# Moving the conversions of a weight matrix between steps of a one-core attention and soft-MoE kernel

## The chip, the cores and the metric

The program runs on one core of a Trainium2 chip. The metric is the device time of one execution in microseconds (us). The kernel before was run three times; its median is 592.17 us (591.44 to 594.74).

## The reference, cut to what matters

```python
# attention: batch 4, heads 12, sequence 448, head dimension 64
scores = cap * np.tanh(scale * np.matmul(q, k.transpose(0, 1, 3, 2)) / cap)
scores = scores - np.max(scores, axis=-1, keepdims=True)
attn = np.exp(scores)
attn = attn / (np.sum(attn, axis=-1, keepdims=True) + 1e-09)
x = (attn @ v) as 1792 tokens x 768
# soft mixture of experts: 8 experts, 4 slots each, 768 -> 1024 -> 768
logits = x @ phi                                  # 1792 x 32
d = softmax of logits over the tokens
slot_input = d.T @ x
slot_out = per expert: np.maximum(slot_input[e] @ w1[e], 0.0) @ w2[e]
x = (softmax of logits over the slots) @ slot_out # 1792 x 768
# MLP: 768 -> 2048 -> 768
h = x @ w_in
g = np.maximum(h, 0.0) + alpha * np.minimum(h, 0.0)
out = g @ w_out
```

The matrices w_in and w_out are stored with 64 bits per number, so the kernel reads each number as two 32-bit words, `lo` and `hi`, and rebuilds a float32 from them.

## The kernel before, in words

**Attention in steps.** Two heads make a pair, so there are 24 pairs. Each pair has four steps, one per block of keys, so the loop runs over steps `g` = 0 to 95 (and two more to drain); `c = g % 4` is the step within the pair. A step issues on TensorE (PE) the score products `s` of one block (six matmuls from the split operands `qh`, `ql`, `kh`, `kl`), then on ScalarE (ACT) a tanh (line 388) and an exp (line 389), and two steps later the product with v (tile `o`). GpSimd (POOL) adds up the exponentials into `acc` (lines 405, 408, 412), six instructions per pair.

**What is prepared ahead.** In the second step of a pair (`c == 1`) the next pair's k and q are transposed on PE (tile `tr`). From the result in PSUM, ACT writes `kh` (line 353), and VectorE (DVE) writes `qh`, `kl` and `ql` (lines 367, 354, 368). Besides that come, as background work due some steps later, the row sums (`rs` on PE, lines 439 and 443 on DVE), every third pair a reciprocal (lines 469 to 471: RECIPROCAL, a cast, and `rh`), the normalisation (`rb` on PE, `xn` on DVE, line 495), the logits (`lg`), the two softmaxes, transposes of x (`nx` on PE, `xnat` on DVE or ACT) and the slot sums (`ss`). The tiles `tr`, `rs`, `rb`, `lg`, `lr`, `nx`, `nd` and `ss` all come out of one PSUM pool of three buffers that are used in rotation: the next one on PE waits until the reader of the third last has done.

**w_in's conversion.** w_in is cut into 24 pieces of 128 by 512 numbers. A piece is loaded by DMA as 64-bit words (512 KB) into one of two buffers of the tile `cvbuf`, rebuilt there by one instruction on ACT (line 185) and four on DVE, and stored to a scratch array (256 KB, line 688) two steps after its conversion; after the store the load of the piece after next is issued (line 668). At which step `g` a piece is converted stands in the list `cv_steps`. The four instructions on DVE are

```python
nc.vector.tensor_scalar(out=t, in0=t, scalar1=H_MIN, scalar2=H_MAX, op0=ALU.max, op1=ALU.min)       # L186
nc.vector.tensor_scalar(out=tu, in0=tu, scalar1=4, scalar2=1, op0=..., op1=...)                      # L190
nc.vector.scalar_tensor_tensor(out=tu, in0=lo, scalar=29, in1=tu, op0=..., op1=...)                  # L193
nc.vector.scalar_tensor_tensor(out=tu, in0=hi, scalar=0x80000000, in1=tu, op0=..., op1=...)          # L196
```

so L186 and L190 read one array, L193 and L196 read two. `order` fixes the order on PE; L185 and L186 are held back until their step. A scheduler arranges the rest of each engine's instructions.

**Expert weights.** While attention runs, `load_next` fetches the first expert weights into slots of a shared area, at the pairs listed in `LOADS`. The eleventh load goes into the slot that `cvbuf` occupies, and so waits for the last store of w_in.

**After attention** come the eight experts, and the MLP with w_in and w_out, both bound to PE.

Of the kernel before, what the change touches and what calls it, by code (L numbers as in the profile page):

```python
# [24 lines left out]
def tile_attention_soft_moe_mlp(ctx, tc, q, k, v, cap, phi, w1, w2, w_in, w_out, alpha, out):  # L25
    nc = tc.nc
    B, H, S, D = q.shape
    J = 4
    P = S // J
    NP = H // 2  # L30
    NPAIR = B * NP
# [8 lines left out]
    HS = S // 2  # L40
# [13 lines left out]
    LOADS = (4, 6, 8, 10, 12, 14, 16, 18, 19, 20, 21, 22)  # L54
# [22 lines left out]
    def slot(i, shape, dtype=F32, name="w"):  # L77
        return arena.tile(shape, dtype, tag=f"slot{i}", name=name)
# [18 lines left out]
    def may_load():  # L97
        if nload[0] == len(loads):
            return None
        late = loads[nload[0]][0] in ("wi", "wo")  # L100
        fit = [n for n in free if not late or n < NA]
        return fit[0] if len(fit) > (late and not kept[0]) else None

    def w1_rows(e, i):

        return w1[e, 384 * i:384 * i + 384, :].rearrange("(p k) f -> p k f", k=3)

    def w2_rows(e, i):

        return w2[e, 512 * i:512 * i + 512, :].rearrange("(j p u) f -> p j u f", p=128, u=2)  # L110

    def load_part(kind, e, i, c, t, after=None):
        if kind == "w2":
            src = w2_rows(e, i)[:, c // 2, c % 2]
        else:
            src = w1_rows(e, i)[:, c]
        ins = nc.sync.dma_start(out=t, in_=src)
        if after is not None:
            tc.add_manual_dep(ins.ins, after.ins.name, NOSYNC, reason="prefetch pace")
        return t  # L120

    def load_next(after=None):
        slot_no = may_load()
        free.remove(slot_no)
        kind, e, i = loads[nload[0]]
        nload[0] += 1
        if slot_no >= NA:

            ts = where.setdefault((kind, e, i), [])
            n = 3 if kind == "w1" else 4  # L130
            for c in range(len(ts), n):
                t = xslots[0].tile([128, SLOT // n], F32, tag=f"slot{slot_no}_{c}", name="w")
                ts.append(load_part(kind, e, i, c, t))
            return
        if kind == "w1":
            t = slot(slot_no, [128, 3, FE])
            src = w1_rows(e, i)
        elif kind == "w2":
            t = slot(slot_no, [128, 4, DM])
            src = w2_rows(e, i)  # L140
        elif kind == "wi":
            t = slot(slot_no, [128, KD, 512])
            src = w_in32[i].rearrange("(k p) f -> p k f", p=128)
        else:
            t = slot(slot_no, [128, 2, DM, 2], U32)
            src = w_out[256 * i:256 * i + 256].rearrange("(k p) f t -> p k f t", p=128)
        if kind == "w1":
            parts = [(t, src)]
        elif kind == "w2":
            parts = [(t[:, 2 * j:2 * j + 2], src[:, j]) for j in range(2)]  # L150
        else:
            parts = [(t[:, c], src[:, c]) for c in range(t.shape[1])]
        if kind == "wo" and i == 0:

            half.append(parts.pop())
        elif kind == "wi" and i == 0:
            parts = [
                (t[:, ks, fs], src[:, ks, fs])
                for fs in (slice(0, 256), slice(256, 512))
                for ks in (slice(0, 3), slice(3, 6))  # L160
            ]
            parts[2:2] = half
        for dst, part in parts:
            ins = nc.sync.dma_start(out=dst, in_=part)
            if after is not None:
                tc.add_manual_dep(ins.ins, after.ins.name, NOSYNC, reason="prefetch pace")
        if kind == "w1":
            t = [t[:, c] for c in range(3)]
        elif kind == "w2":
            t = [t[:, c] for c in range(4)]  # L170
        where[kind, e, i] = t
        held[kind, e, i] = slot_no
# [61 lines left out]
    def attention():  # L234
        with ExitStack() as pools:
# [27 lines left out]
            phi_sb = ac0_p.tile([128, KD, NSLOT], F32, name="phi")  # L263
# [13 lines left out]
            nat, stk, sc_t, pt, acc, ov, xu, xn = {}, {}, {}, {}, {}, {}, {}, {}  # L277
# [7 lines left out]
            def matmul(*a, **kw):  # L285
                ins = nc.tensor.matmul(*a, **kw)  # L286
                if order:
                    if order[0] is not None:
                        tc.add_manual_dep(ins.ins, order[0].ins.name, NOSYNC, reason="tilings together")
                    order[0] = ins  # L290
                return ins
# [8 lines left out]
            def aux(shape, name):  # L300
                if now[0] > NPAIR * J and name in ("nx", "ss"):
                    return ps_s.tile([128, 2, 512], F32, tag="s", name=name)[:, 0, :][:shape[0], :shape[1]]
                return ps_a.tile([128, 512], F32, tag="a", name=name)[:shape[0], :shape[1]]
# [212 lines left out]
            def logits(b, part):  # L516

                if part != 1:
                    lps[b] = aux([128, S], "lg")
                ps = lps[b]  # L520
                pairs = range(NP) if part is None else range(GP) if part == 0 else range(GP, NP - 1)
                end = pairs.stop if part != 0 else NP - 1
                for m in pairs:
                    r = 32 * (m % 4)
                    matmul(
                        ps[r:r + 32, :],
                        phi_sb[:, m, :],
                        xn[b * NP + m],
                        start=(m < 4),
                        stop=(m + 4 >= end),  # L530
                        tile_position=(0, r),
                    )
                if part == 0:
                    return
                ls = sm_p.tile([128, S], F32, tag="ls", name="ls")
                if part is None:
                    nc.vector.tensor_copy(out=ls, in_=ps)
                else:
                    nc.scalar.activation(out=ls, in_=ps, func=AF.Copy)
                if part is None:  # L540
                    later(2, softmax_d, b, ls)
                    for m in range(2):
                        later((2 if b < B - 2 else 4) + m, nat_x, b * NP + m)
                    return
                norm(NPAIR - 1, sums[NPAIR // GP - 1], True)
                for m in range(5):
                    nat_x(b * NP + m)
                lps[b] = aux([128, S], "lr"), ls
                matmul(lps[b][0], stackI, ls, start=True, stop=False)
                for m in range(3):  # L550
                    nat_x(b * NP + m)
                last_logits()
# [117 lines left out]
            ncv = KD * (DFF // 512)  # L670


            cv_steps = [4, 7, 10, 13, 16, 19, 22, 25, 29]
            while len(cv_steps) < ncv:
                cv_steps.append(cv_steps[-1] + J)

            def cv_at(n):
                return cv_steps[n]
# [39 lines left out]
            last = None  # L718
            for g in range(NPAIR * J + LAG):
                now[0] = g  # L720
                i, c = divmod(g, J)
                if g == 14:
                    nc.sync.dma_start(out=alpha_sb, in_=alpha.rearrange("(k p) -> p k", p=128))
                if g == 17:
                    nc.vector.tensor_scalar(out=nalpha_sb, in0=alpha_sb, scalar1=-1.0, scalar2=None, op0=ALU.mult)
                if i < NPAIR:
                    qk(i, CHUNKS[c])
                    if c == 1 and i + 1 < NPAIR:
                        trans_k(i + 1)
                        trans_q(i + 1)  # L730
                run_bg()
                if i < NPAIR:
                    if c == 0:
                        last = load(i + 2, "kq") or last
                    for n in range(ncv):
                        if cv_at(n) == g - 2:
                            store_w_in(n)
                        if cv_at(n) == g:
                            conv_w_in(n)
                    if c == 3 and i in LOADS and may_load() is not None:  # L740
                        load_next(last)
                if g >= LAG:
                    n, e = divmod(g - LAG, J)
                    pv(n, CHUNKS[e])
                    if e == J - 1:
                        load(n + 2, "v")
            order.clear()
            while bg:
                now[0] += 1
# [8 lines left out]
            ps = aux([128, KD * NSLOT], "si").rearrange("p (k s) -> p k s", k=KD)  # L758
# [611 lines left out]
```

## Time and profile before

| | before |
|---|---|
| median of three runs | 592.17 us (591.44 to 594.74) |
| the profiled execution | 591.62 us |
| its span | 589.7 us |
| mean granted clock of TensorE | 0.991 |
| PE busy | 94% of the span |
| DVE, ACT, POOL busy | 74%, 64%, 29% |

The span is what the profiler recorded of the program; the execution's own time is 1.9 us longer. Busy shares are averages over three stages of different kind: attention (to about 255 us), experts, MLP. POOL works in attention alone. The pairs are counted from 0. Pair p's stretch is taken from the start of its first tanh to that of the next pair, and the windows below have these borders: pair 2 begins at 28.27 us, pairs 3, 4 and 5 at 36.44, 46.32 and 56.52, pair 6 at 66.63, pair 13 at 133.16, pair 21 at 217.24 and pair 23 at 238.65.

### The profile page before, as it was taken

The page shows a single profiled execution, that of the slowest core. Times are in us where ns is not written, and L with a number is a line of the kernel's source. Part 1 is how long each engine was busy: PE and PEld are TensorE (multiplying, and loading weights), DVE is VectorE, ACT ScalarE, POOL GpSimd, SP SyncE. Part 2 cuts the span into 40 slices and gives each one's busy share as a digit, 9 for nine tenths or more (in the row PEclk, how much of TensorE's full clock was granted, in tenths as well). Part 3 has the DMA queues.
Part 4 walks back from the last instruction along what each step waited for, and adds up shares of the span by engine and source line. Part 5 has one row for each costly group of instructions (what it writes and reads, how often), then busy time and mean ns, then how long its engine had stood idle before and what let it go on. Part 6 is the DMA issues. An engine that isn't in the chain of part 4 may idle for free.

```text
span 589.7 us, 10780 instructions
## 1 busy us (share of the span) xinstructions
PE 557.1 (94%) x4008; PEld 385.1 (65%) x4008; DVE 437.7 (74%) x834; ACT 377.0 (64%) x617; POOL 173.1 (29%) x158
## 2 busy tenths in 40 slices
PE   5998999999999999989888899999999999999996
PEld 4443444445444545454445568878888999999996
DVE  3699798896769768451012399999999979797974
ACT  3997999798988878620011167764787855555651
POOL 0799588767585755500000000000000000000000
PEclk9999999999999999997999999999999999999999
DMA  7668788798887971899999999300120101010101
GB/s 177 128 183 285 197 241 260 211 241 260 245 246 197 323 233 51 306 360 412 419 421 418 391 400 416 116 0 1 42 67 1 55 0 54 2 53 1 54 1 54
DMA packets 83460, 110.92 MB, mean 188 GB/s; under 512 B 55376, under 2 KB 63312, under 8 KB 81872
## 3 DMA queue, kind: packets, MB, share of 16 engines
q1 hardware_dynamic: 81168, 109.28, 55.9%
q10 hardware_dynamic: 2240, 0.95, 0.6%
q8 instruction: 32, 0.52, 0.4%
q14 instruction: 20, 0.16, 0.1%
HBM read 98.41 MB, written 11.80 MB: 187 GB/s over the span
## 4 chain that ended last, share of the span: by engine, by line
PE 78%; DVE 9%; ACT 6%; DMA 3%; issue 2%; SPq 1%; ACTq 0%; DVEq 0%
PE o L286 9%; PE s L286 8%; PE P L1196 7%; PE P L1194 6%; PE P L1195 6%; PE oc L969 6%; PE oc L975 6%; PE oc L976 6%; PE y L860 5%; PE h L836 4%; PE aps L897 2%; PE nx L286 2%; ACT p L389 2%; PE rs L286 2%; ACT p L388 2%
## 5 line engine op out<-in xcount | busy, mean ns | idle before, releaser
L286 PE MATMUL o<-p,v 128*64 128x448 f32 (+1 forms) x384 | 94.0, 568 | 3.2 <-ACT xu L414 2.6
L388 ACT ACTIVATE p<-s 128x896 f32<-128x896 f32 x96 | 78.6, 819 | 23.7 <-PE s L286 20.7
L389 ACT ACTIVATE p<-p,cap 128x896 f32<-128x896 f32 x96 | 91.0, 948 | 2.2
L405 POOL TENSOR_TENSOR acc<-p 128x448 f32<-128x448 f32 x48 | 60.1, 1273 | 59.0 <-ACT p L389 59.0
L975 PE MATMUL oc<-wsp,gr 128*128 128x512 f32 (+1 forms) x192 | 64.8, 338 | 0.0
L976 PE MATMUL oc<-wsp,gr 128*128 128x512 f32 (+1 forms) x192 | 64.1, 337 | 0.0
L286 PEld LDWEIGHTS s<-qh,kh 64*128 64x128 f32 (+1 forms) x168 | 18.3, 187 | 68.5 <-issue 26.1
L969 PE MATMUL oc<-wsp,gr 128*128 128x512 f32 (+1 forms) x192 | 61.9, 339 | 0.0
L1185 ACT ACTIVATE gr<-gs 128x384 fp32r<-128x384 f32 (+1 forms) x64 | 36.7, 576 | 32.8 <-DVE gs L1169 26.9
L408 POOL TENSOR_TENSOR acc<-acc,p 64x448 f32<-64x448 f32 x46 | 55.3, 1203 | 1.7
L412 POOL TENSOR_TENSOR acc<-acc,p 128x448 f32<-128x448 f32 x46 | 54.7, 1209 | 1.8
L1186 DVE TENSOR_TENSOR gr<-gs,gr 128x384 fp32r<-128x384 f32 x64 | 39.2, 619 | 17.5 <-ACT gr L1185 17.5
L286 PE MATMUL s<-qh,kh 64*128 64x448 f32 (+1 forms) x168 | 46.2, 476 | 1.2 <-DVE qh L367 1.2
L1194 PE MATMUL P<-wsp,gr 128*128 128x384 f32 x128 | 42.9, 335 | 0.0
L1196 PE MATMUL P<-wsp,gr 128*128 128x384 f32 x128 | 42.8, 334 | 0.0
L1195 PE MATMUL P<-wsp,gr 128*128 128x384 f32 x128 | 42.8, 334 | 0.0
L975 PEld LDWEIGHTS oc<-wsp,gr 128*128 128x128 f32 x192 | 36.4, 189 | 5.1 <-DVE wx L196 0.4
L969 PEld LDWEIGHTS oc<-wsp,gr 128*128 128x128 f32 x192 | 36.2, 190 | 5.4 <-ACT wsp L804 0.8
L976 PEld LDWEIGHTS oc<-wsp,gr 128*128 128x128 f32 x192 | 36.3, 189 | 4.4 <-issue 0.4
L286 PE MATMUL s<-ql,kh 64*128 64x448 f32 (+1 forms) x168 | 35.7, 368 | 1.7 <-DVE ql L368 1.7
L286 PEld LDWEIGHTS o<-p,v 128*64 128x64 f32 (+1 forms) x384 | 19.0, 134 | 27.9 <-issue 11.6
L847 ACT ACTIVATE small<-h 128x256 f32<-128x256 f32 x8 | 4.9, 610 | 48.6 <-PE h L836 48.6
(234 smaller groups left out, 1267.2 us busy)
## 6 DMA issues: line engine op xcount, KB each, us to landing
w<-in_moe_w_dram SPq DMA_DIRECT2D x26, 768.0 KB, 9.9
w<-in_moe_w_dram SPq DMA_DIRECT2D x12, 1536.0 KB, 9.4
cvbuf<-in_moe_w_in_dram SPq DMA_DIRECT2D x24, 512.0 KB, 4.8
w<-in_moe_w_out_dram SPq DMA_DIRECT2D x16, 768.0 KB, 10.4
w_in<-cvbuf SPq DMA_DIRECT2D x24, 256.0 KB, 2.7
w<-in_moe_w_dram SPq DMA_DIRECT2D x12, 512.0 KB, 6.0
q<-in_q_dram SPq DMA_DIRECT2D x44, 112.0 KB, 3.7
k<-in_k_dram SPq DMA_DIRECT2D x48, 96.0 KB, 5.0
```

Source lines behind the costliest of these rows:

```text
L286: ins = nc.tensor.matmul(*a, **kw)
L388: nc.scalar.activation(out=pe, in_=ps[:, :n, :S], func=AF.Tanh)
L389: nc.scalar.activation(out=pe, in_=pe, func=AF.Exp, scale=cap_sb)
L405: nc.gpsimd.tensor_add(out=a[:, u, :], in0=pt[i, 0][:, u, :], in1=pe[:, u, :])
L408: nc.gpsimd.tensor_add(out=a[r, u, :], in0=a[r, u, :], in1=pt[i, JK][r, 0, :])
L412: nc.gpsimd.tensor_add(out=a[:, u, :], in0=a[:, u, :], in1=pe[:, u, :])
L969: ins = nc.tensor.matmul(o, gh[:, ts], wo_h[f][:, cols], start=(f == 0 and not second), stop=False)
L975: nc.tensor.matmul(o, gh[:, ts], wo_l[f][:, cols], start=False, stop=False)
L976: nc.tensor.matmul(o, gl[:, ts], wo_h[f][:, cols], start=False, stop=(f == KF - 1 and not more))
L1194: nc.tensor.matmul(o, hi[:, i], bh, start=(p == 0), stop=False)
L1195: nc.tensor.matmul(o, hi[:, i], bl, start=False, stop=False)
L1196: nc.tensor.matmul(o, lo[:, i], bh, start=False, stop=(p == 7))
```

## The change

Three things change. First, the list of conversion steps. Before, piece 0 is converted at step 4, then one every third step to 25, then 29 and every fourth step to 89; from 25 on each is at a pair's second step. After, the steps are 3, 6, every fourth step from 9 to 49 (second steps), every third step from 52 to 67, and 71, 74, 77, 80, 83. Second, an expert load that a pair of `LOADS` issues comes at the end of the pair's second step in place of its fourth, ahead of the product with v. Third, in the logits of the first three batches the products of pairs 4 and 5 of the batch are cut into two halves of 224 columns, which go to all four groups of 32 rows of the result.

```diff
-                    r = 32 * (m % 4)
-                    matmul(
-                        ps[r:r + 32, :],
-                        phi_sb[:, m, :],
-                        xn[b * NP + m],
-                        start=(m < 4),
-                        stop=(m + 4 >= end),
-                        tile_position=(0, r),
-                    )
+                    halves = part is None and m >= 4
+                    for h in range(2 if halves else 1):
+                        r = 32 * (2 * (m - 4) + h if halves else m % 4)
+                        cols = slice(h * HS, h * HS + HS) if halves else slice(0, S)
+                        matmul(
+                            ps[r:r + 32, cols],
+                            phi_sb[:, m, :],
+                            xn[b * NP + m][:, cols],
+                            start=(m < 4),
+                            stop=halves or (part is not None and m + 4 >= end),
+                            tile_position=(0, r),
+                        )
...
-            cv_steps = [4, 7, 10, 13, 16, 19, 22, 25, 29]
-            while len(cv_steps) < ncv:
-                cv_steps.append(cv_steps[-1] + J)
+            cv_steps = [3, 6] + list(range(9, 50, J)) + list(range(52, 68, 3)) + [71, 74, 77, 80, 83]
...
-                    if c == 3 and i in LOADS and may_load() is not None:
-                        load_next(last)
...
+                if i < NPAIR and c == 1 and i in LOADS and may_load() is not None:
+                    load_next(last)
```

On DVE, in pair 4 (steps 16 to 19), piece 4 stands before in the middle of the reciprocal and in front of `qh` of the next pair:

```order
L469 RECIPROCAL sums<-sums 128x224
L470 CAST rh<-sums 128x224
L186 TENSOR_SCALAR cvbuf<-cvbuf 128x512
L471 SCALAR_TENSOR_TENSOR rh<-rh,masks,sums 128x224
L190 TENSOR_SCALAR cvbuf<-cvbuf 128x512
L193 SCALAR_TENSOR_TENSOR cvbuf<-cvbuf 128x512
L196 SCALAR_TENSOR_TENSOR cvbuf<-cvbuf 128x512
L367 TENSOR_SCALAR qh<-tr,tscale 128x448
L354 TENSOR_TENSOR kl<-tr,kh 128x512
L368 SCALAR_TENSOR_TENSOR ql<-tr,tscale,qh 128x448
```

At the same place of the changed kernel the DVE's rows are these:

```order
L469 RECIPROCAL sums<-sums 128x224
L470 CAST rh<-sums 128x224
L471 SCALAR_TENSOR_TENSOR rh<-rh,masks,sums 128x224
L367 TENSOR_SCALAR qh<-tr,tscale 128x448
L354 TENSOR_TENSOR kl<-tr,kh 128x512
L368 SCALAR_TENSOR_TENSOR ql<-tr,tscale,qh 128x448
L186 TENSOR_SCALAR cvbuf<-cvbuf 128x512
L190 TENSOR_SCALAR cvbuf<-cvbuf 128x512
```

The piece has moved behind the three splits, to step 17. On DVE in pair 13 (steps 52 and 53), before, the reciprocal and the splits stand without a conversion between them:

```order
L469 RECIPROCAL sums<-sums 128x224
L495 TENSOR_TENSOR xn<-xu,rb 128x448
L470 CAST rh<-sums 128x224
L471 SCALAR_TENSOR_TENSOR rh<-rh,masks,sums 128x224
L367 TENSOR_SCALAR qh<-tr,tscale 128x448
L354 TENSOR_TENSOR kl<-tr,kh 128x512
L368 SCALAR_TENSOR_TENSOR ql<-tr,tscale,qh 128x448
L186 TENSOR_SCALAR cvbuf<-cvbuf 128x512
```

In the changed kernel DVE has at this place:

```order
L469 RECIPROCAL sums<-sums 128x224
L495 TENSOR_TENSOR xn<-xu,rb 128x448
L470 CAST rh<-sums 128x224
L186 TENSOR_SCALAR cvbuf<-cvbuf 128x512
L471 SCALAR_TENSOR_TENSOR rh<-rh,masks,sums 128x224
L190 TENSOR_SCALAR cvbuf<-cvbuf 128x512
L193 SCALAR_TENSOR_TENSOR cvbuf<-cvbuf 128x512
L367 TENSOR_SCALAR qh<-tr,tscale 128x448
L196 SCALAR_TENSOR_TENSOR cvbuf<-cvbuf 128x512
L354 TENSOR_TENSOR kl<-tr,kh 128x512
L368 SCALAR_TENSOR_TENSOR ql<-tr,tscale,qh 128x448
```

Here a conversion has come in among the reciprocal and the splits; the same happens in pair 16 (step 64). On PE the third logits, in pair 20, stood as six products (each listed row is one matmul of the program, which the trace shows as two instructions):

```order
-L286 MATMUL lg<-xn,phi 32x448 x6
+L286 MATMUL lg<-xn,phi 32x448 x4
+L286 MATMUL lg<-xn,phi 32x224 x4
```

Two of the six are now four, of half the columns each.

## Rows read from the trace of the kernel before

**Rows 1.** The page's first part: busy us, share of the span, instructions.

```profile
PE 557.1 (94%) x4008; PEld 385.1 (65%) x4008; DVE 437.7 (74%) x834; ACT 377.0 (64%) x617; POOL 173.1 (29%) x158
```

**Rows 2.** Windows by pairs: length; busy us by engine (instructions); clock, DMA share, GB/s.

```profile
28.27:36.44 8.17, 8.17 (x55) 3.78 (x55) 8.00 (x10) 8.07 (x12) 7.30 (x7) 1.00 0.60 166
36.44:46.32 9.88, 9.52 (x58) 4.08 (x57) 9.74 (x10) 8.82 (x13) 9.73 (x8) 1.00 0.76 214
46.32:56.52 10.20, 7.73 (x50) 3.67 (x51) 10.03 (x15) 8.23 (x13) 9.14 (x8) 0.99 0.86 270
56.52:66.63 10.11, 10.11 (x56) 4.80 (x57) 8.93 (x12) 8.27 (x12) 5.33 (x5) 0.84 0.87 253
66.63:101.75 35.12, 34.54 (x221) 16.33 (x222) 29.66 (x39) 33.45 (x46) 30.12 (x25) 1.00 0.80 237
...
133.16:217.24 84.08, 82.31 (x598) 41.05 (x600) 61.76 (x109) 71.43 (x100) 56.15 (x49) 1.00 0.85 252
217.24:238.65 21.41, 20.38 (x164) 10.72 (x163) 16.68 (x32) 18.42 (x27) 13.69 (x12) 1.00 0.29 83
```

**Rows 3.** Timeline of DVE from 47 us: start, us, instruction, idle before.

```profile
48.68 0.41 DVE L186 TENSOR_SCALAR cvbuf<-cvbuf 128x512 f32<-128x512 f32 x1
...
50.27 1.36 DVE L190 TENSOR_SCALAR cvbuf<-cvbuf 128x512 uint32<-128x512 uint32 x1
...
52.39 1.51 DVE L196 SCALAR_TENSOR_TENSOR cvbuf<-cvbuf 128x512 uint32<-128x512 uint32 x1
53.83 0.67 DVE L367 TENSOR_SCALAR qh<-tr,tscale 128x448 fp32r<-128x448 f32 x1
```

**Rows 4.** Timeline of PE over the same stretch.

```profile
47.35 0.55 PE L286 MATMUL tr<-ident,q 112*128 112x112 f32 x4
...
54.65 0.47 PE L286 MATMUL s<-qh,kh 64*128 64x448 f32 x2 [1.19 <-DVE qh L367]
55.74 0.47 PE L286 MATMUL s<-ql,kh 64*128 64x448 f32 x2 [0.62 <-DVE ql L368]
```

**Rows 5.** Windows of one microsecond.

```profile
57.00:58.00 1.00, 1.00 (x5) 0.30 (x4) 0.96 (x2) 0.97 (x2) 0.92 (x2) 0.50 1.07 413
```

**Rows 6.** The tile cvbuf on DVE: duration min/median/max in ns over all 24 pieces.

```profile
L190 DVE TENSOR_SCALAR cvbuf<-cvbuf x24: 415/428/1359, 21.8 to 233.3; 128x512 uint32<-128x512 uint32 x24
L196 DVE SCALAR_TENSOR_TENSOR cvbuf<-cvbuf x24: 679/694/1527, 25.1 to 235.0; 128x512 uint32<-128x512 uint32 x24
```

**Rows 7.** Timeline of POOL in pairs 12 and 13.

```profile
130.54 2.38 POOL L405 TENSOR_TENSOR acc<-p 128x448 f32<-128x448 f32 x2 [2.26 <-ACT p L389]
...
135.40 2.28 POOL L412 TENSOR_TENSOR acc<-acc,p 128x448 f32<-128x448 f32 x2
140.32 2.47 POOL L405 TENSOR_TENSOR acc<-p 128x448 f32<-128x448 f32 x2 [2.64 <-ACT p L389]
```

**Rows 8.** Timeline of DVE in pairs 13 and 14.

```profile
134.35 1.22 DVE L471 SCALAR_TENSOR_TENSOR rh<-rh,masks,sums 128x224 fp32r<-128x224 f32 x1
136.03 0.68 DVE L367 TENSOR_SCALAR qh<-tr,tscale 128x448 fp32r<-128x448 f32 x1 [0.46 <-PE tr L286]
136.63 0.68 DVE L354 TENSOR_TENSOR kl<-tr,kh 128x512 fp32r<-128x512 f32 x1
...
137.88 0.43 DVE L186 TENSOR_SCALAR cvbuf<-cvbuf 128x512 f32<-128x512 f32 x1
...
147.15 0.69 DVE L367 TENSOR_SCALAR qh<-tr,tscale 128x448 fp32r<-128x448 f32 x1 [1.53 <-PE tr L286]
```

**Rows 9.** Timeline of PE in pair 13.

```profile
138.07 0.65 PE L286 MATMUL nx<-ident,xn 128*112 128x128 f32 x4
```

**Rows 10.** Timeline of PE in pair 20: the third logits.

```profile
208.30 1.70 PE L286 MATMUL lg<-xn,phi 128*32 128x448 f32 x12
```

**Rows 11.** Timeline of SP, the DMA queue: the eleventh expert load.

```profile
237.77 0.81 SPq L164 DMA_DIRECT2D w<-in_moe_w_dram  x2
```

**Rows 12.** Waits from 238 to 345 us: in total, times, longest; the one for a DMA.

```profile
DVE wsp L805 <- DMA w<-in_moe_w_dram: 1.0, 1, 1.0
```

## The prediction, made before the changed kernel was run

> **What bounds the kernel now.** I read the page first: PE is busy in 94% of the span [rows 1], so a gain has to be a place where PE stands still, runs at a lower clock, or has too much work; a loss is a new one. Then I cut attention into windows by pairs [rows 2] and looked for pairs that take longer than their PE work. A steady pair, without softmax work, takes 8.78 us (pairs 6 to 9: 35.12 / 4) and pair 2 takes 8.17. Pairs 3, 4 and 5 take 9.88, 10.20 and 10.11. In pairs 3 and 4 DVE is busy for 9.74 of 9.88 and 10.03 of 10.20 us: DVE is the bound there, and PE works in only 7.73 of pair 4's 10.20. In pair 5 PE is busy throughout, but its granted clock is 0.84.
>
> The timelines show how. In pair 4 the last q transpose ends at 47.90 (47.35 + 0.55) [rows 4], but DVE writes `qh` only at 53.83 [rows 3], because piece 4 stands in front of it. PE then waits 1.19 us for `qh` and 0.62 for `ql` [rows 4], and right behind this the granted clock is 0.50 for a while [rows 5]: 1.2 instead of 2.4 GHz.
>
> Why DVE is late has two parts. A conversion comes every third step, and each is dear. L190 takes 428 ns in the median, and 1.36 us here; L196 694 ns, and 1.51 here [rows 3, 6]. POOL is busy in 9.73 of 9.88 us of pair 3 and 9.14 of 10.20 of pair 4 [rows 2]. Later each conversion sits at the second step, and POOL rests just there: in pair 13 POOL ends at 137.68 and starts again at 140.32 [rows 7], and the conversion starts at 137.88 with 0.43 for L186 [rows 8]. So the price of a conversion depends on whether POOL works beside it: about 2.2 us free (0.41 + 0.43 + 0.69 + 0.69, taking L193 like L196), and 1.75 us more beside POOL (0.93 for L190, 0.82 for L196).
>
> **The change, part by part.**
>
> *Early pieces.* Pieces 2 to 12 now stand at second steps, as those of pairs 6 to 9 do. DVE then no longer falls behind in pairs 3 to 5, PE's waits go, and with them the low clock. If the three pairs take 8.78 each, the gain is 30.19 - 26.34 = 3.85 us; if pairs 3 and 4, which have little normalisation yet, come at 8.17, it is 5.07. I take 4.5. Pieces 0 and 1 come a step earlier, in the first pairs, where POOL has little to do; nothing.
>
> *Late pieces.* From step 52 on they come every third step. In pairs 13 to 20 that is 11 pieces where there were 8. Eight of the 11 (52, 55, 64, 67, 71, 74, 80, 83) do not follow the splits in POOL's pause; I count 74 because the work of step 71 pushes it back. DVE is busy for 61.76 of 84.08 us there now [rows 2]. It gets 3 x 2.2 + 8 x 1.75 = 20.6 us more, 82.4 in all, or 98%, the share at which pair 4 stood. The bound from below is nothing: the work would just fit. The bound from above is the early price: in pairs 3 to 5 three pieces away from second steps (16, 19, 22) cost 4.5 us, 1.5 each, so eight cost 12.
>
> Between them I go by places. Step 52 has the pattern of the early place: the conversion in the middle of the reciprocal and in front of the splits. There `rh` starts at 134.35 and takes 1.22; `qh` starts at 136.03, `kl` ends at 137.31, and PE's `nx` at 138.07 takes the buffer that `kl` frees, with 0.76 us to spare [rows 8, 9]. Now L186 (0.4), L190 and L193 beside POOL (1.36 + 0.7 to 1.5) and L196 (0.7) come in ahead of `kl`: 3.2 to 4.0 us. Of that DVE's idle time of 0.46 before `qh` and the 0.76 to spare are covered: a stall of 2.0 to 2.7 us, which PE cannot make up because it works in 82.31 of 84.08 us [rows 2]. Queued behind the waiting `nx` on PE are the next `o` and `s`, and so ACT. Step 64 repeats it: I take 2.2 us for each, 4.4. For five others (55, 67, 71, 80, 83) I take half of the early price, 0.75 each, 3.75, since DVE has pauses there, such as 1.53 us in front of `qh` at 147.15 [rows 8]; 74 I leave at nothing. Sum 8.2 us.
>
> The rows give 1.75 us as the surcharge of a piece beside POOL. The Trainium skill, page "SBUF — State Buffer", section "SBUF: two separate sides", says that VectorE operations in a two-port mode or with two SBUF inputs and GpSimd's share a port pair as an exclusive lock, held for a whole instruction by whichever started first. The trace agrees in kind: L190 and L196 grow by 0.93 and 0.82, under one POOL instruction (2.28 / 2 = 1.14). By that rule the worst piece would wait for one in front of L190, L193 and L196, 3.4 us, and the eight pieces would ask for 13 us more of DVE than I count; no row shows a piece as dear throughout.
>
> *Pieces taken away from steps 85 and 89.* They ran where DVE has room (16.68 busy of 21.41 us) and PE is busy for 20.38 [rows 2]: nothing.
>
> *Logits in halves.* The twelve instructions of one batch take 1.6 us [rows 10]: two rounds of 0.8 over the row groups, the second half empty. Two halves on four groups save 0.4 per batch, 1.2 in three batches, if the groups run beside each other; nothing where row sums fill the empty groups already. I take 0.8.
>
> *Expert loads.* Earlier issue, on an SP queue that takes the stores and loads of the pieces too. The eleventh load, issued at 237.77 [rows 11], can go after the store of step 85, into a stretch where DMA is busy for 0.29 of the time [rows 2]. But nobody on PE waits for a DMA from 238 to 345 us; the one such wait is 1.0 us on DVE [rows 12]. I take nothing, at best a gain of 1.0. The cover is PE's own work in the expert stage.
>
> *Sum.* 591.6 - 4.5 + 8.2 - 0.8 = 594.5 us for an execution like the profiled one. The median of before lies 0.55 above that execution, so **595 us**. The measurement tells 0.5%, about 3 us, from no change: below 589.2 is faster, above 595.1 slower.
>
> **Rivals.**
>
> *The late pieces are hidden (faster).* PE and ACT have work queued and DVE's 22.3 us of idle time in pairs 13 to 20 takes the 20.6 us. Then -4.5 - 0.8 and 0 to 2 for what is left: 587 to 589. For it: the 98% is an upper sum, if less of a piece meets POOL, and before shows conversions near `nx` without a stall. Against it: the early pairs lost time at the same share. It decides where the late cost is under 2.9 us.
>
> *Gain and loss cancel.* With single stalls only at 52 and 64 (4.4), the sum is 590.7, some 591 in the median: no change. It also holds if the early pairs gain nothing and the late ones lose nothing.
>
> *The clock falls again (slower still).* The early waits of 1.19 + 0.62 us were followed by the low clock, which made pair 5 cost 10.11 instead of 8.78. Stalls of 2 us at 52 and 64 could do the same, 1.3 us each, and with the late price at its upper end of 12 the time is 591.6 - 5.3 + 12 + 2.6 + 0.5 = 601.
>
> **How the numbers follow.** Forecast, a late cost of 5 to 12 us (591.5 to 598.5): 0.45, of which 0.2 inside 0.5%. Hidden, 587 to 589: 0.30. Cancelled, about 591: 0.10. Clock, 599 to 603: 0.15. So faster 0.30, same 0.30, slower 0.40. The range for 8 in 10 leaves out most of the last case and the lower edge of the second: 587 to 600. The forecast's own range is 591.5 to 598.5.
>
> **What would show it.** Right: pairs 3, 4 and 5 at 8.2 to 8.8 us with a clock of 1.00; in pairs 13 to 20 together some 92 us instead of 84, DVE at 0.9 or more, L190 at over 1 us at steps 52 and 64, and PE waiting for `kl` or an `nx` waiting there; 217 to 239 us unchanged in length. Wrong: pairs 13 to 20 within 2 us of 84.08 with conversions between POOL's instructions at the free price, or pairs 3 to 5 still above 9.5 us, which would mean that something other than the conversions held DVE back.

## The result, and the profile after

The changed kernel takes 599.45 us in the median of four runs (597.66 to 600.50), against 592.18 before; the ratio is 1.0112, with a 95% interval of 1.0073 to 1.0151. It is slower, as forecast, and by more: 7.3 us where 2.8 were expected (595 against 592.17). The profiled execution took 597.66 us, its span is 595.9 us, 6.2 more than before.

The windows with the borders of the pairs (columns as in [rows 2]) show that a gain and a loss stand against each other. The first row is pairs 3 to 5, the second pairs 13 to 20, the third pair 21, the last one microsecond of it:

```profile
36.89:62.87 25.98, 25.09 (x162) 11.67 (x161) 22.39 (x30) 24.80 (x33) 22.61 (x19) 1.00 0.78 234
128.59:219.80 91.21, 82.99 (x606) 40.85 (x608) 78.12 (x117) 72.96 (x104) 61.26 (x49) 1.00 0.76 228
219.80:234.61 14.81, 11.54 (x83) 5.82 (x83) 11.14 (x20) 8.58 (x13) 6.93 (x6) 0.88 0.65 208
227.00:228.00 1.00, 1.00 (x4) 0.00 (x0) 0.49 (x2) 0.00 (x0) 0.00 (x0) 0.50 0.00 0
```

Pairs 3 to 5 take 25.98 us where they took 30.19. Pairs 13 to 20 take 91.21 where they took 84.08 [rows 2]. Pair 21 takes 14.81, and 11.07 before (217.24 to 228.31). At the start of pair 13 the changed kernel is 4.57 us ahead (128.59, not 133.16). At the start of pair 22 it is 6.30 behind (234.61, not 228.31), and it stays there.

PE's waits from 128 to 245 us, with their totals, times and longest, show where it stands still:

```profile
PE nd L286 <- DVE kl L354: 3.3, 1, 3.3
PE ss L286 <- DVE xnat L510: 1.7, 2, 1.0
PE o L286 <- ACT xu L414: 1.5, 1, 1.5
PE lr L286 <- DVE xn L495: 1.4, 1, 1.4
PE nx L286 <- DVE xn L495: 1.3, 1, 1.3
PE rs L286 <- DVE kl L354: 0.6, 1, 0.6
PE tr L286 <- DVE xnat L510: 0.5, 1, 0.5
```

With three of 0.3 that are not shown these make 11.2 us; in the kernel before PE waited for 2.4 us over pairs 13 to 22. Every row but one names DVE, and the one that names ACT (`o` for `xu`) is DVE's too: ACT had been waiting 1.66 us for DVE's `xn`. The 8.8 us more, and 1.7 us from windows with a low clock in pair 21 (0.58, 0.50, 0.50, 0.71 from 226 to 230), come to 10.5 us; pairs 13 to 21 lost 10.9, from which the logits had already taken some 0.7 off (pairs 16 and 20, below).

The timeline of DVE in front of the longest wait shows the last piece (step 83) ahead of the splits `qh` and `kl`:

```profile
218.83 1.23 DVE L186 TENSOR_SCALAR cvbuf<-cvbuf 128x512 f32<-128x512 f32 x1 [0.24 <-ACT cvbuf L185]
220.09 1.25 DVE L190 TENSOR_SCALAR cvbuf<-cvbuf 128x512 uint32<-128x512 uint32 x1
...
222.28 0.68 DVE L193 SCALAR_TENSOR_TENSOR cvbuf<-cvbuf 128x512 uint32<-128x512 uint32 x1
222.99 1.50 DVE L196 SCALAR_TENSOR_TENSOR cvbuf<-cvbuf 128x512 uint32<-128x512 uint32 x1
224.53 0.68 DVE L367 TENSOR_SCALAR qh<-tr,tscale 128x448 fp32r<-128x448 f32 x1
225.13 0.68 DVE L354 TENSOR_TENSOR kl<-tr,kh 128x512 fp32r<-128x512 f32 x1
```

On PE the transposes `nd` follow, which need the buffer that `kl` frees, and the third logits, now sixteen instructions, stand in pair 20:

```profile
211.21 1.34 PE L286 MATMUL lg<-xn,phi 128*32 128x448 f32 x16
...
225.95 0.46 PE L286 MATMUL nd<-ident,ls 64*112 64x64 f32 x4 [3.27 <-DVE kl L354]
```

The piece costs 4.66 us there (1.23 + 1.25 + 0.68 + 1.50). The logits take 1.34 us where they took 1.70 [rows 10].

### The profile page after: what moved, and what is told of

Read it like the earlier page. It is cut to its first block, busy times and chain, and to the rows that moved or that the text cites. A ratio compares the mean times of both kernels' runs of the same rounds, so it can differ in the third digit from the quotient of the medians.

```text
span 595.9 us, 10805 instructions
## 1 busy us (share of the span) xinstructions
PE 556.5 (93%) x4020; PEld 384.5 (65%) x4020; DVE 449.7 (75%) x834; ACT 376.8 (63%) x617; POOL 177.6 (30%) x158
## 4 chain that ended last, share of the span: by engine, by line
PE 72%; DVE 12%; ACT 8%; DMA 4%; issue 2%; SPq 1%; ACTq 0%; DVEq 0%
PE o L286 8%; PE P L1197 6%; PE P L1195 6%; PE P L1196 6%; PE s L286 6%; PE oc L970 6%; PE oc L976 6%; PE oc L977 6%; PE y L861 5%; PE h L837 4%; ACT p L389 2%; PE aps L898 2%; ACT p L388 2%; DVE cvbuf L193 2%; DVE cvbuf L196 2%
## 5 line engine op out<-in xcount | busy, mean ns | idle before, releaser
L405 POOL TENSOR_TENSOR acc<-p 128x448 f32<-128x448 f32 x48 | 62.2, 1316 | 60.7 <-ACT p L389 60.7
L412 POOL TENSOR_TENSOR acc<-acc,p 128x448 f32<-128x448 f32 x46 | 56.4, 1246 | 1.8
L286 PEld LDWEIGHTS o<-p,v 128*64 128x64 f32 (+1 forms) x384 | 19.0, 134 | 28.8 <-ACT xu L414 10.5
L286 PE MATMUL s<-qh,kl 64*128 64x448 f32 (+1 forms) x168 | 35.7, 367 | 0.0
```

What stands on the lines that cost most here:

```text
L405: nc.gpsimd.tensor_add(out=a[:, u, :], in0=pt[i, 0][:, u, :], in1=pe[:, u, :])
L412: nc.gpsimd.tensor_add(out=a[:, u, :], in0=a[:, u, :], in1=pe[:, u, :])
```

## The experiments

**The early part alone** (e1_early_part):

```diff
-            cv_steps = [4, 7, 10, 13, 16, 19, 22, 25, 29]
-            while len(cv_steps) < ncv:
-                cv_steps.append(cv_steps[-1] + J)
+            cv_steps = [3, 6] + list(range(9, 50, J)) + list(range(53, 94, J))
```

> The kernel before with the early part of the new list alone: pieces at steps 3, 6, every fourth step from 9 to 49, and on at second steps from 53 to 93; loads and logits as before. Theory (the conversion steps make both the gain and the loss): pairs 3 to 5 take some 8.6, 8.6 and 8.8 us, pairs 13 to 20 stay at about 84 us, and the time is 588 us (587 to 589.5). The last piece is four steps later than before, so the eleventh expert load is issued later too. Rival (the expert load matters): what is gained early is lost again behind 245 us in waits for a DMA, and the time is 591 us or more.

593.15 us, ratio 1.0007 (0.9983 to 1.0032): no change. Pairs 3 to 5 take 25.99 us, pairs 13 to 21 95.16 (before 95.15), and pair 23 starts 2.8 us earlier than before (235.81). But from there to the end it takes 3.5 us more. The waits from 236 to 350 us name what the kernel before did not have there:

```profile
PE h L834 <- DMA w<-in_moe_w_dram: 3.6, 2, 2.1
PEld h L834 <- DMA w<-in_moe_w_dram: 2.6, 1, 2.6
PEld y L858 <- DMA w<-in_moe_w_dram: 2.5, 2, 1.4
PE y L858 <- DMA w<-in_moe_w_dram: 1.5, 2, 0.9
```

So the rival came true. The eleventh load, behind the last store, was issued at 244.12 us, not 237.77 [rows 11], and the experts then wait for their weights. The list cannot be put right early by pushing all its pieces later.

**The late part alone** (e3_late_part):

```diff
-            cv_steps = [4, 7, 10, 13, 16, 19, 22, 25, 29]
-            while len(cv_steps) < ncv:
-                cv_steps.append(cv_steps[-1] + J)
+            cv_steps = [4, 7, 10, 13, 16, 19, 22, 25] + list(range(29, 46, J)) + list(range(52, 68, 3)) + [71, 74, 77, 80, 83]
```

> The kernel before with the late part of the new list alone: pieces 0 to 12 at the steps of before, the others at 52, 55, 58, 61, 64, 67, 71, 74, 77, 80, 83; loads and logits as before. Theory: pairs 3 to 5 cost 30.2 us as before, pairs 13 to 20 take 7 us more than 84.1 and pair 21 some 3.7 more than 11.1, so that the time is 602.5 us (601 to 605). Rival (loads or logits make a part of the loss of the changed kernel): this kernel loses clearly less, and the time is 599 us or under.

607.33 us, ratio 1.0238 (1.0194 to 1.0282), more than expected. Pairs 13 to 21 take 107.53 us, 12.4 more than before; pair 21 alone 14.84. The rest of the 16.5 us by which its span grew lies in places that the edit does not touch: pairs 2 to 5 take 1.9 us more than in the profile of before, pair 10 1.3, and the part behind pair 23's start 1.4 (in that part the length differs by as much between kernels that do the same there, see the last section). The late list makes the loss without help from the logits or the loads.

**The logits alone, and the loads alone** (e4_halves_alone, e5_loads_alone). The edits are the first and the last hunk of the change.

> The kernel before with the logit products of pairs 4 and 5 of the first three batches in halves, nothing else. Theory: 0.4 us less in each of three batches at most, so the time is 591.4 us (590.9 to 592.2), and the third logits take 1.3 us in place of 1.62. Rival: the row sums filled the empty row groups already, and nothing changes (592.2, pairs 10, 16 and 20 as before).

> The kernel before with the expert loads at the end of a pair's second step, nothing else. Theory: no PE instruction waits for these transfers, and the time stays at 592.2 us (591.6 to 592.8). Rival: the loads now meet the pieces' loads and stores in the DMA queue, conversions or transposes start late, and the time is 593.5 us or more; or an earlier eleventh load gains 1 us behind attention.

The logits: 591.72 us, ratio 0.9978 (0.9952 to 1.0004), which the runs cannot tell from no change. The profile can: pairs 16 and 20 take 9.92 and 12.79 us where they took 10.26 and 13.15, some 0.35 us less in each, and the candidates below show the same (9.90 to 9.92 and 12.79 to 12.80). The loads: 592.41 us, ratio 0.9989 (0.9966 to 1.0011): no change.

**POOL's additions cut short, in the kernel before and in the changed one** (e6_short_pool_before, e7_short_pool_after). The same edit in both:

```diff
-                    acc[i] = acc_p[i % 2].tile([128, 2, S], F32, tag="acc", name="acc")
+                    acc[i] = accs[i % 2]
...
-                        nc.gpsimd.tensor_add(out=a[:, u, :], in0=pt[i, 0][:, u, :], in1=pe[:, u, :])
+                        nc.gpsimd.tensor_add(out=a[:, u, :W], in0=pt[i, 0][:, u, :W], in1=pe[:, u, :W])
```

with `W = 56`, and likewise in lines 408 and 412; `accs` are two tiles set to one at the start.

> The kernel before with POOL's six additions per pair cut from 448 to 56 columns; the other columns of acc keep a constant, so the sums of the softmax are left out but for an eighth. The order of DVE's instructions stays. Theory (conversions are dear because POOL works beside them): every conversion takes 2.2 us, pairs 3, 4 and 5 take 8.3 to 8.8 us each, and attention ends some 4 us earlier, so the time is 588 us. Rival (a conversion every third step in front of the splits is late by its place, whatever POOL does): pairs 3 to 5 still take 29 us or more together, and the time is 591 us or more.

> The changed kernel with POOL's six additions per pair cut to 56 columns in the same way. Theory: the late conversions cost 2.2 us each in place of 3.97, so that most of the 10.9 us which pairs 13 to 21 lose goes; they take 98 to 99 us in place of 106.0 (before: 95.15), and the time is 588 to 591.5 us, at most 3.5 us over the kernel before with short additions. Rival (place and order of the pieces on DVE make the loss): pairs 13 to 21 still take 103 us or more, and the time is 595 us or more.

The first takes 590.41 us (0.9955, 0.9929 to 0.9982), the second 587.41 (0.9896, 0.9857 to 0.9936). With POOL's work cut to a quarter (16.92 us in pairs 13 to 21 of e7 in place of 68.19), the changed kernel is the faster one. The windows are pairs 3 to 5 and pairs 13 to 21 of e6:

```profile
36.91:63.24 26.33, 25.96 (x167) 12.01 (x165) 18.69 (x33) 24.91 (x35) 6.26 (x18) 1.00 0.79 243
129.37:224.37 95.00, 92.38 (x679) 46.38 (x681) 65.74 (x128) 80.78 (x114) 16.26 (x54) 1.00 0.78 234
```

and pairs 13 to 21 of e7:

```profile
129.04:222.72 93.68, 91.47 (x687) 46.46 (x689) 69.79 (x136) 81.16 (x116) 16.92 (x55) 1.00 0.83 251
```

The conversions of e7 on DVE (min/median/max, ns, as in [rows 6]):

```profile
L190 DVE TENSOR_SCALAR cvbuf<-cvbuf x24: 421/427/429, 20.0 to 211.1; 128x512 uint32<-128x512 uint32 x24
L196 DVE SCALAR_TENSOR_TENSOR cvbuf<-cvbuf x24: 681/691/694, 24.6 to 213.1; 128x512 uint32<-128x512 uint32 x24
```

In e6 pairs 3 to 5 lose next to nothing (26.33 us) although a piece comes every third step. In e7 pairs 13 to 21 take 93.68 us in place of 106.02 (91.21 + 14.81), less than in e6 (95.00, without the logits in halves). No conversion takes longer than the free price. The order of the pieces on DVE is that of the kernel before and of the changed one. So both losses are made by POOL working beside DVE, and the place in front of the splits hurts only at the dear price. The edit makes other work on DVE cheaper too (`rh`, last section); the conversions alone take 39.8 us of DVE in pairs 13 to 21 of the changed kernel, 24.5 in e7 and, with two pieces fewer, 20.2 in the kernel before. The profiled executions fell by less than attention gained, since the part behind pair 23's start takes 2.0 us more in e6's profile and 2.9 in e7's (last section).

**The last piece at step 85** (e8_last_piece_at_85):

```diff
-            cv_steps = [3, 6] + list(range(9, 50, J)) + list(range(52, 68, 3)) + [71, 74, 77, 80, 83]
+            cv_steps = [3, 6] + list(range(9, 50, J)) + list(range(52, 68, 3)) + [71, 74, 77, 80, 85]
```

> The changed kernel with the last piece at step 85 in place of 83, behind the splits of pair 21 and not in front of them. Theory: PE's wait of 3.3 us for kl in pair 21 and the low clock after it go, pair 21 takes 11.1 us as before, and the time is 595.7 us (595 to 596.5). Rival: the wait comes from the pieces before it (80 and the logits), pair 21 still takes 13 us or more, and the time is 598 us or more.

Pair 21, in one window:

```profile
220.55:231.62 11.07, 10.04 (x83) 5.34 (x83) 9.13 (x20) 9.20 (x14) 6.25 (x6) 1.00 0.62 176
```

It is back at 11.07 us with a clock of 1.00: the low clock of pair 21 is gone and PE's wait for `kl` is 1.0 us as in the kernel before, so both losses were the one piece's. The profiled execution took 594.66 us, 3.0 less than that of the changed kernel. The median of six runs is 598.17 (1.0107, 1.0067 to 1.0146), only 1.3 less, the two intervals overlap, and the time is the rival's (598 or more) though the pair is not. Two of the six had a lower mean clock (0.985 and 0.988) than any run of the changed kernel (0.990 to 0.993); what the last piece is worth in the median stays open.

**A version that keeps the last step** (e2_candidate): logits in halves, and

```diff
-            cv_steps = [4, 7, 10, 13, 16, 19, 22, 25, 29]
-            while len(cv_steps) < ncv:
-                cv_steps.append(cv_steps[-1] + J)
+            cv_steps = [3, 6] + list(range(9, 86, J)) + [87, 89]
```

> The kernel before with the early list of the change, second steps from 9 to 85, and 87 and 89 for the last two pieces, so that the last one keeps its step of before; logits in halves; loads as before. Theory: pairs 3 to 5 gain 3.8 us, the logits 0.7, step 87 costs nothing because POOL rests there, and the transfers behind attention end earlier by as much as attention does; the time is 588 us (587 to 589.5). Rival (the expert stage then waits for transfers, as with a last piece at 93): attention ends 4 us earlier, but waits for a DMA take 2 us or more behind it, and the time is 590 us or more.

590.97 us, ratio 0.9966 (0.9938 to 0.9994): faster, but short of 588. That is the rival's time, but not for its reason: no instruction on PE waits for a DMA behind attention. Pair 22 takes 14.49 us, not 10.34, because the piece at 87 met the reciprocal and the splits, as piece 4 did in the kernel before. The timeline of DVE:

```profile
221.14 1.55 DVE L469 RECIPROCAL sums<-sums 128x224 f32<-128x224 f32 x1
222.61 0.70 DVE L186 TENSOR_SCALAR cvbuf<-cvbuf 128x512 f32<-128x512 f32 x1
223.24 1.22 DVE L470 CAST rh<-sums 128x224 fp32r<-128x224 f32 x1
224.38 0.41 DVE L190 TENSOR_SCALAR cvbuf<-cvbuf 128x512 uint32<-128x512 uint32 x1
224.72 1.32 DVE L471 SCALAR_TENSOR_TENSOR rh<-rh,masks,sums 128x224 fp32r<-128x224 f32 x1
225.97 1.64 DVE L193 SCALAR_TENSOR_TENSOR cvbuf<-cvbuf 128x512 uint32<-128x512 uint32 x1
```

and on PE the wait that follows:

```profile
229.66 0.62 PE L286 MATMUL nx<-ident,xn 128*112 128x128 f32 x4 [2.64 <-DVE kl L354]
```

Behind it the clock is 0.50 in the window from 232 to 233. My expectation that POOL rests at step 87 was wrong.

**The one piece too many in other places** (e10_extra_at_59, e11_extra_at_23). Both like e2_candidate, with

```diff
-            cv_steps = [3, 6] + list(range(9, 86, J)) + [87, 89]
+            cv_steps = [3, 6] + list(range(9, 58, J)) + [59] + list(range(61, 90, J))      # e10
+            cv_steps = [3, 6] + list(range(9, 22, J)) + [23] + list(range(25, 90, J))      # e11
```

> The kernel before with pieces at 3, 6, every second step of a pair from 9 to 89, and one more at step 59, in pair 14; logits in halves; loads as before. Theory (a piece costs where it runs beside POOL in front of the splits, unless DVE has idle time there): pairs 3 to 5 take 26.0 us, pairs 14 and 15, where DVE idles some 6 us in the kernel before, at most 1 us more than before (18.4), pair 22 10.3; the time is 587.5 us (586.5 to 589.5). Rival: the piece at 59 makes a buffer late as that at step 87 did, pairs 14 and 15 take 20.5 us or more, and the time is 590 us or more.

> The same with the one more piece at step 23, in pair 5, in place of 59. Theory: DVE idles some 2.4 us in each of pairs 5 and 6, a piece beside POOL takes 4.0, so the two pairs take at most 0.5 us more than 17.6, and the time is 587.5 us (586.5 to 589). Rival: the piece at step 25 comes two steps after the store that frees its buffer, ACT waits for its load, and pairs 5 and 6 take 19 us or more; the time is 589.5 us or more.

e10 takes 589.27 us, ratio 0.9952 (0.9931 to 0.9974), faster than both kernels. Pairs 14 and 15, in one window, take 1.1 us more than before (18.4), and pairs 3 to 5 take 25.98:

```profile
140.05:159.54 19.49, 18.12 (x131) 9.01 (x131) 16.85 (x23) 17.40 (x24) 13.47 (x12) 1.00 0.79 241
```

e11 takes 593.20 us (1.0019, 0.9993 to 1.0045). Its rival came true, and more: pair 6 alone takes 15.10 us. ACT waits for the load of the piece at step 25, PE then 4.3 us for ACT's `xu`, and the clock falls for some 7 us (70 to 77 us). The rows are ACT's timeline and one of these windows:

```profile
70.84 0.66 ACT L185 ACTIVATE cvbuf<-cvbuf 128x512 f32<-128x512 f32 x1 [4.10 <-DMA cvbuf<-in_moe_w_in_dram]
...
73.00:74.00 1.00, 1.00 (x4) 0.33 (x4) 0.83 (x2) 0.81 (x1) 0.11 (x1) 0.50 1.25 305
```

## Why the prediction was right, and where its sizes were off

The direction came as forecast, and in the main both mechanisms. The time of 599.45 us lies within the wide range (587 to 600) by 0.55 us only, and outside the forecast's own (591.5 to 598.5). It falls where I had put the falling clock (599 to 603); that came once, at another step than I named, and for 1.7 us, so the clock alone does not explain the time.

Of the signs that I named, these came: pairs 3 to 5 at 8.6 to 8.8 us with a clock of 1.00, L190 at 1.36 and 1.37 us at steps 52 and 64, and pairs 13 to 20 at 91.21 us ("some 92"). DVE at 0.9 did not, and from pair 21 to pair 23, where I expected no change from 21.41 us, it takes 25.15 (219.80 to 244.95).

**Early pieces: right.** Forecast 4.5 us, between 3.85 and 5.07; pairs 3 to 5 gained 4.21. e6 shows that the loss before needs POOL beside DVE: the same list loses next to nothing there when POOL is quiet. e1 and e10 repeat the figure (25.99 and 25.98). One reading was wrong. I wrote that POOL rests at the second steps. In pairs 6 to 9 it does not: there a piece took 3.7 to 3.9 us in the kernel before, as this one of pair 8 shows,

```profile
89.32 1.26 DVE L190 TENSOR_SCALAR cvbuf<-cvbuf 128x512 uint32<-128x512 uint32 x1
90.61 0.69 DVE L193 SCALAR_TENSOR_TENSOR cvbuf<-cvbuf 128x512 uint32<-128x512 uint32 x1
91.34 1.51 DVE L196 SCALAR_TENSOR_TENSOR cvbuf<-cvbuf 128x512 uint32<-128x512 uint32 x1
```

and still each of these pairs took 8.8. In pairs 3 to 5 of the changed kernel a piece takes 3.3 to 4.0 us. So those pairs did not gain by free conversions: there are three where there were four, and each stands behind the splits.

**Late pieces: right in kind, too small in sum.** I took 8.2 us; pairs 13 to 21 lost 10.9 in the profiled execution, or 11.6 without the 0.7 of the logits, and 12.4 in e3. The mechanism is shown by e7. The distribution over the places was wrong. Steps 52 and 64, for which I had worked out stalls of 2.0 to 2.7 us, cost less than the 2.2 each that I took: pair 13 lost 1.36, pair 14 0.54 (with step 55) and pair 16 0.30 (0.64 without the logits), and no single wait of PE there is longer than 0.8 us. Step 80 cost nothing. Steps 67 and 71, with 0.75 each, cost more: pair 17 lost 1.24 and pair 18 1.22. I left the piece at 74 "at nothing", and pair 19, behind it, lost 2.82, with waits of PE of 1.32 us for `xn` and 0.95 for `xnat`. I gave the piece at 83 "half of the early price", 0.75, and pair 21 lost 3.74: PE's wait for `kl` grew from 1.0 to 3.3 us, and the clock took 1.7, which I had put into a rival and at steps 52 and 64. Steps 74 and 83 cost 5.8 us more than I gave them, steps 67 and 71 1.0 more, the others 3.4 less: 3.4 us were missing in the sum. That pairs 13 to 20 came near "some 92" is in part luck, as too much at some places stood against too little at others. e8 shows the part of step 83.

**DVE at 98%: wrong.** DVE was busy for 78.12 of 91.21 us, 86%. The price of a piece was not the error. Of the eight that I had counted, seven took 3.7 to 4.7 us (the four instructions together) and that at step 80 2.6, 4.06 on average, or 1.84 over the free 2.22; I took 1.75. But the last one ran almost wholly in pair 21, so that pairs 13 to 20 got 16.4 us more and not 20.6, and they grew longer by 7.1 us. PE lost time long before DVE was full, because one late `kl`, `xn` or `xnat` holds a shared buffer.

**The port rule.** The Trainium skill, page "SBUF — State Buffer", section "SBUF: two separate sides", has VectorE's instructions with two SBUF inputs, or in a two-port mode, and GpSimd's exclude each other for whole instructions. e6 and e7 agree: with short additions the longest L196, which reads two arrays, falls from 1,537 to 694 ns. No run here tells in which mode L186 and L190, which read one, work. The splits, which read PSUM, take 0.67 to 0.68 us in all these timelines. The 3.4 us that I worked out by it for the worst piece show in no late piece: those from step 52 on cost at most 2.5 us over the free price. The piece at step 3 of the changed kernel, with all four instructions dear, comes near (5.5 us, 3.3 over it).

**Logits: right.** Forecast 0.8 us for three batches; pairs 16 and 20 gained 0.34 and 0.36 in e4. (I worked with 1.6 us for the twelve instructions; the row says 1.70.) The first batch (pair 10) was not settled, since that pair takes 9.9 to 11.9 us from kernel to kernel.

**Expert loads: right for this change, with a limit that I had not seen.** e5 shows no effect. But e1 shows that the cover ends right behind the kernel before: a last store some 6 us later makes PE wait for its weights.

**The median.** The three executions that were not profiled took 599.4 to 600.5 us, some 2 to 3 us more than the profiled one. Their mean clock (0.990 to 0.993, and 0.991 in the profiled one) does not explain it. Nothing here shows where the time went; it stays open, and with it some 1.2 of the 4.4 us by which the median missed 595. The other 3.2 are the profiled execution's (597.66, not 594.5), and the late pieces' 3.4 us are their main term.

## What to carry to other kernels

Put VectorE's work between arrays in SBUF into GpSimd's pauses, or price it with GpSimd beside it: here 3.7 to 4.7 us late in attention instead of 2.2. Then see what stands behind it on VectorE: in pairs 6 to 9 a dear piece cost nothing, in front of the splits or of `xn` it did. An engine's idle share does not tell whether a delay on it is free; look for who holds the buffer that the bound engine needs next. A stall of the bound engine can cost about half its length again through the clock that follows: here 1.7 us beside a wait of 3.3.

## What the runs showed that I had not expected

L186, with one operand from SBUF and one result there, is held up by POOL too: the longest of the changed kernel took 1,226 ns and the shortest 408, while e7's longest is 429. So is the cast of the reciprocal, 1.22 us in e2_candidate and 0.27 in the changed kernel at 129.47 us, and so is `rh` (L471), which takes 1.21 to 1.33 us each time in the changed kernel and 0.45 in e7.

A wait of PE of 2.6 us (e2_candidate), 3.3 us (the changed kernel) and 4.3 us (e11) went with a clock of 0.50, the lower of the two levels, each time (in e11 it fell within the wait, which runs from 67.6 to 72.0 us, at 70.0); steps 52 to 74 with waits of at most 1.5 us did not: there every window shows 1.00. Early, in the kernel before, 1.19 and 0.62 us close together were enough [rows 4, 5].

Behind attention the clock is 0.50 for a while in every profile but e1's, and for one of two lengths. In e10 ten windows in a row show it, from 260 to 270 us; the first and the last are

```profile
260.00:261.00 1.00, 1.00 (x28) 1.00 (x22) 0.27 (x1) 0.00 (x0) 0.00 (x0) 0.50 1.04 415
269.00:270.00 1.00, 1.00 (x16) 0.49 (x12) 0.00 (x0) 0.00 (x0) 0.00 (x0) 0.50 0.91 346
```

In the kernel before and the changed one there are six in a row. The profiles with six (these two, e2, e4, e8) need 350.8 to 351.1 us from the start of pair 23 to the end of the span, those with nine or ten (e3, e5, e6, e7, e10, e11) 352.4 to 353.9. Three or four us more at half the clock would cost 1.5 to 2, about that difference; e7, the longest, has a second such stretch, of some 3 us, from 336 us. The length does not follow the edits: e5, which leaves the work there as it is, has the long one. So 1.5 us of what one profile differs from another is no effect of a kernel here, and it hides a part of what e6, e7 and e10 gained in attention. Why a run gets the one or the other stays open.

The executions that were not profiled differ in the clock too. Of the 75 runs of the kernel before that were taken beside the experiments, the eight with a mean clock of 0.995 or more took 588.8 to 590.3 us, the 19 with 0.988 or less 593.2 to 596.9. Where in those runs the clock was low is not shown.
